# Linear attention and feed-forward on one core: w and u as single rows spread by PE, decay blocks by fp32 matmuls, a shared PSUM pool, unit loads one by one, weight slices gated one by one, dummy matmuls first

## The chip, the cores and the metric

The kernel runs on one core of a Trainium2 chip. The metric is the device time of one execution in microseconds (us), median of several runs. The engines are named as in the profile: PE (matmuls), PEld (weight loads of PE), DVE, ACT, POOL, SP; "SPq" and "POOLq" or a DMA_DIRECT2D row on POOL are the queues of an engine in the act of issuing a DMA.

## The reference

The reference is a linear-attention recurrence, followed by a feed-forward layer with a squared ReLU (cut to what matters):

```python
# r, k, v: (4, 8, 768, 48); w, u: (8, 48); w_in: (384, 2048); w_out: (2048, 384); all fp32
for t in range(S):
    cur = np.einsum('bhd,bhe->bhde', u[None] * kt, vt)
    y[:, :, t] = np.einsum('bhd,bhde->bhe', rt, state + cur)      # (r.(u*k)) v is the "diagonal" term
    state = w[None, :, :, None] * state + np.einsum('bhd,bhe->bhde', kt, vt)
...
h = np.maximum(x @ w_in, 0.0)          # x: y as 3072 tokens x 384
out = h * h @ w_out
```

## The kernel before

The sequence is cut into 24 units (6 chunks of 128 tokens, 4 batches). For a unit, r and k are scaled by decay tables (`Wt2`, `Wkhat`, from log w), transposed, and multiplied into a masked score block; PE forms Y and the state update; DVE adds the diagonal term `dv = v * sum(r*u*k)`. Two units make a group of 256 tokens for the feed-forward layer: eight hidden steps (L604, six matmuls each), and four output steps per unit (L638, four matmuls each). The eight weight slices (four of w_in, four of w_out) are cast to bf16 by DMAs that POOL issues.

The program does not fix the order of these steps by hand. It lists them as `Step`s with guessed durations, simulates the engines in `order_steps`, and emits the instructions in the order of the simulated starts. A buffer holds a pair of units:

```python
        else:                                   # a single unit's load
            x, i = item[0], int(item[1:])
            var = f"{x}P{i // 2}"
            def go(x=x, i=i, var=var):
                nc.sync.dma_start(out=ld[x][slot[var]][:, i % 2], in_=single[x][i % B, i // B])
            Ld[x, i] = st("ld" + item, "SP", 0.4, dma=1.04, prio=-150 + n, emit=go,
                          alloc=[(var, "ld" + x)] if i % 2 == 0 else [])
...
PLAN = dict(..., loads=['k0', 'r0', 'v0', 'ub', 'k1', 'r1', 'v1', 'wcol', 'kP1', 'rP1', 'vP1', 'kP2', ...],
            nprep=8, p1set=2, nT=8, nX=8, gates=[('v', 2), ('v', 2)], ...)
POOLS = dict(ldr=2, ldk=2, ldv=2, rk=6, P0=4, dv=3, vb=8, rkT=6, bank=3, bankH=3, bankO=2, ...)
```

Only units 0 and 1 are loaded singly here (`k0` ... `v1`); `kP1` is both units of pair 1 in one DMA. w comes as a broadcast to 128 partitions (`wb`, 192 KB), u likewise (`ub`), and once more as a column (`wcol`). `gates` says which load has to land before POOL issues weights: v of unit 2 for both halves.

## Time and profile before

| | before |
|---|---|
| timed median | 183.56 us (183.44 to 183.97) |
| profiled span | 180.6 us |
| PE busy | 160.6 us (89%) |
| first hidden-layer matmul | 27.48 us |
| first weight slice issued | 18.23 us |
| DMA packets under 512 B | 98,864 of 105,794 |

The page's second part, the span in 40 slices of 4.5 us, with the busy share of PE, the granted PE clock and the DMA engines in tenths:

```profile
PE   0344769899999999999999999999999999999991
PEclk9999999999999999999999999999999999999999
DMA  3999999999949649979799799897896255221102
```

PE is full from the eighth slice or so, and DMA from the second. The table of stretches (start and end in us, length, then busy us and instruction counts of PE, PEld, DVE, ACT, POOL, then clock, DMA share and GB/s) makes this exact:

```profile
0.00:27.40 27.40, 12.47 (x128) 8.62 (x129) 20.84 (x44) 10.89 (x18) 16.50 (x29) 1.00 0.99 182
27.40:38.30 10.90, 9.82 (x111) 7.95 (x109) 9.84 (x18) 10.14 (x19) 4.25 (x5) 1.00 1.26 187
38.30:177.10 138.80, 138.26 (x1357) 101.67 (x1356) 97.92 (x156) 95.98 (x179) 86.01 (x84) 1.00 0.74 153
```

From 38.3 us on, PE is idle for half a microsecond in all. What can be won is in the start. The timeline there (start us, us, engine, line, operation, tiles; in brackets the idle time before and what ended it):

```profile
17.66 0.63 POOL L364 COPY gate<-ldv 1x1 f32<-1x1 f32 x2
...
18.23 3.26 POOL L371 DMA_DIRECT2D W<-in_moe_w_in_dram  x4
...
23.21 0.61 PE L454 MATMUL bank<-rkT 48*128 48x128 bf16 x8 [1.10 <-ACT rkT L436]
...
27.48 1.83 PE L604 MATMUL bank<-xT,W 128*128 128x256 bf16 x12
...
29.25 0.40 PE L454 MATMUL bank<-rkT 48*128 48x128 bf16 x8
```

The gates open at 17.7 us, all eight weight slices are issued by 24.5, the first hidden step runs at 27.5. The two L454 lines are the same work, eight score matmuls, first at 0.61 us, six microseconds later at 0.40.

**PE time lost.** "Busy" hides slow and dummy matmuls, so I use a second measure below. Each kind of useful matmul gets the time by which it advances a busy PE, read from the timeline of this kernel late in the span: a hidden matmul 0.655/6 us, an output matmul 0.65/4, and the attention's small ones 0.03 to 0.057. Summed over the trace this is 152.5 us of work (151.6 in the changed kernel, which does two transposes fewer on PE). At a time t, "lost" is t minus the useful work begun by then. These are estimates from the trace, good to some tenths of a us. The kernel before has lost 16.7 us by 20 us, 23.4 by 45, and 24.4 at its end.

### The profile page before, as it was taken

To read this page: it belongs to the slowest core of one execution; us is meant where nothing else is said; L and a number is where in the kernel's file an instruction comes from. 1 tells how busy PE (TensorE), PEld (TensorE's weight loads), DVE (VectorE), ACT (ScalarE), POOL (GpSimd) and SP (SyncE) were. 2 spreads that over 40 slices of the span, in tenths; PEclk is the share of its full clock that TensorE was granted. 3 is DMA by queue.
4 is the path that set the end of the run, shared out by engine and by line. 5 is a ranking of instruction groups with operands and counts; after the bars stand their busy time and mean duration, and the time that the engine had idled before them with its cause. 6 is when DMAs were issued, how large, how long until landed. Compare 5 with 4: busy or idle time off the path is not lost.

```text
span 180.6 us, 4082 instructions
## 1 busy us (share of the span) xinstructions
PE 160.6 (89%) x1592; PEld 118.2 (65%) x1592; DVE 128.6 (71%) x216; ACT 117.5 (65%) x214; POOL 106.8 (59%) x116
## 2 busy tenths in 40 slices
PE   0344769899999999999999999999999999999991
PEld 0222557778766867758678677677686776777760
DVE  3399998997388838959979696778777889631310
ACT  2641528986793886827776758579298495496851
POOL 2346998024940999599879977986968980000000
PEclk9999999999999999999999999999999999999999
DMA  3999999999949649979799799897896255221102
GB/s 85 207 195 216 196 191 193 184 185 222 225 116 241 149 82 253 184 152 241 142 216 204 122 237 202 138 225 164 167 228 155 71 120 80 65 65 47 41 2 87
DMA packets 105794, 28.44 MB, mean 157 GB/s; under 512 B 98864, under 2 KB 105776, under 8 KB 105776
## 3 DMA queue, kind: packets, MB, share of 16 engines
q1 hardware_dynamic: 102064, 25.04, 68.1%
q0 software_dynamic: 3712, 3.15, 11.0%
q8 instruction: 12, 0.20, 0.5%
q14 instruction: 6, 0.05, 0.1%
HBM read 20.84 MB, written 4.72 MB: 142 GB/s over the span
## 4 chain that ended last, share of the span: by engine, by line
PE 79%; DVE 9%; DMA 4%; ACT 2%; SPq 2%; issue 1%; DVEq 0%
PE bank L638 34%; PE bank L604 32%; PE bank L454 4%; PE bank L483 3%; DMA ub<-in_u_dram 2%; DMA xT<-xs 2%; PE bank L478 2%; PE bank L429 2%; DVE rk L382 2%; SPq L351 2%; DVE xs L506 2%; DVE dv L411 2%; PE bank L495 2%; DVE Bm L467 1%; ACT rkT L436 1%
## 5 line engine op out<-in xcount | busy, mean ns | idle before, releaser
L618 ACT ACTIVATE hr<-bank 128x512 bf16<-128x512 f32 x96 | 55.9, 595 | 29.4 <-PE bank L604 27.6
L604 PE MATMUL bank<-xT,W 128*128 128x256 bf16 x576 | 73.8, 273 | 0.4 <-DVE hq L629 0.3
L638 PE MATMUL bank<-W,hq 128*128 128x384 bf16 x384 | 72.0, 326 | 0.0
L604 PEld LDWEIGHTS <-W 128*128 128x128 bf16 x576 | 55.0, 98 | 11.8 <-issue 0.9
L638 PEld LDWEIGHTS <-hq 128*128 128x128 bf16 x384 | 36.1, 98 | 19.3
L629 DVE TENSOR_TENSOR hq<-bank,hr 128x512 bf16<-128x512 f32 x48 | 32.6, 683 | 17.4 <-ACT hr L618 17.4
L467 DVE TENSOR_TENSOR Bm<-bank,maskJT 128x512 bf16<-128x512 f32 x48 | 31.1, 681 | 8.2 <-PE bank L454 8.1
L388 POOL TENSOR_TENSOR P<-ldr,ldk 128x384 f32<-128x384 f32 x24 | 28.2, 1177 | 9.9 <-DMA ldr<-in_r_dram 9.9
L528 POOL TENSOR_TENSOR S0W<-ts,WLm 128x384 bf16<-128x384 f32 x16 | 16.5, 1031 | 29.1 <-DVE ts L522 28.9
L626 ACT ACTIVATE hq<-hr 128x512 bf16<-128x512 bf16 x48 | 30.2, 630 | 1.1
L397 POOL TENSOR_TENSOR P<-P,ub 128x384 f32<-128x384 f32 x22 | 22.9, 1043 | 1.4
L411 DVE TENSOR_TENSOR dv<-ldv,du 128x384 f32<-128x384 f32 x24 | 21.2, 883 | 0.5
L506 DVE TENSOR_TENSOR xs<-bank,dv 128x384 bf16<-128x384 f32 x24 | 13.3, 555 | 11.1 <-PE bank L483 10.7
L651 ACT COPY os<-bank 128x384 f32<-128x384 f32 x24 | 11.4, 476 | 12.4 <-PE bank L638 12.1
L429 PE MATMUL bank<-identity,rk 128*128 128x128 bf16 x64 | 7.5, 273 | 10.5 <-DVE rk L382 10.2
L382 POOL TENSOR_TENSOR rk<-ldr,Wt 128x384 bf16<-128x384 f32 x16 | 16.6, 1040 | 0.1
L382 POOL TENSOR_TENSOR rk<-ldk,Wkhat 128x384 bf16<-128x384 f32 x16 | 16.0, 1002 | 0.0
L429 PEld LDWEIGHTS <-rk 128*128 128x128 bf16 x64 | 5.5, 120 | 12.4 <-DVE rk L382 11.5
L417 ACT CAST vb<-ldv 128x384 bf16<-128x384 f32 x24 | 11.6, 507 | 2.9 <-DMA ldv<-in_v_dram 2.9
L403 DVE TENSOR_REDUCE du<-P 128x8 f32<-128x384 f32 x24 | 13.0, 543 | 0.2 <-POOL P L397 0.2
L454 PE MATMUL bank<-rkT 48*128 48x128 bf16 x192 | 10.6, 233 | 2.5 <-ACT rkT L436 2.2
L483 PE MATMUL bank<-vb,Bm 128*128 128x48 bf16 x192 | 12.2, 189 | 0.4 <-DVE Bm L467 0.4
(40 smaller groups left out, 101.7 us busy)
## 6 DMA issues: line engine op xcount, KB each, us to landing
out_dram<-os SPq DMA_DIRECT2D x24, 192.0 KB, 2.6
ldk<-in_k_dram SPq DMA_DIRECT2D x11, 384.0 KB, 4.1
ldr<-in_r_dram SPq DMA_DIRECT2D x11, 384.0 KB, 5.0
ldv<-in_v_dram SPq DMA_DIRECT2D x11, 384.0 KB, 4.0
W<-in_moe_w_in_dram POOLq DMA_DIRECT2D x4, 384.0 KB, 8.9
W<-in_moe_w_out_dram POOLq DMA_DIRECT2D x4, 384.0 KB, 15.6
ldk<-in_k_dram SPq DMA_DIRECT2D x2, 192.0 KB, 4.2
ldr<-in_r_dram SPq DMA_DIRECT2D x2, 192.0 KB, 4.5
```

The costliest lines, as they stand in the source:

```text
L382: e.tensor_mul(rk[slot[f"rk{i}"]][:, j, :, 0:D], ld[x][slot[f"{x}P{i // 2}"]][:, i % 2], tab)
L388: nc.gpsimd.tensor_mul(P0b[slot[f"P0{i}"]], ld["r"][slot[f"rP{i // 2}"]][:, i % 2], ld["k"][slot[f"kP{i // 2}"]][:, i % 2])
L397: (nc.vector if eng == "DVE" else nc.gpsimd).tensor_mul(t, t, ub)
L411: nc.vector.tensor_mul(dvb[slot[f"dv{i}"]], ld["v"][slot[f"vP{i // 2}"]][:, i % 2], du_b)
L454: nc.tensor.matmul(heads(f"bA{i}{e}", "bank", 128)[:, hc, :], rkT[p0 : p0 + D, HP + hc, :], rkT[p0 : p0 + D, hc, :], start=True, stop=True ...
L467: nc.vector.tensor_mul(Bmb[slot[f"Bm{i}"]][:, e], heads(f"bA{i}{e}", "bank", 128), mask_b)
L483: nc.tensor.matmul(Y[:, hc, D * e : D * (e + 1)], Bm[:, e, hc, :], vb[:, 2 * hc + e, :], start=(c == 0), stop=True, skip_group_check=True,)
L604: nc.tensor.matmul(hp[:, fi, :], W1[s // 2][:, c, 128 * f : 128 * (f + 1)], xt[:, c, :], start=(c == 0), stop=(c == CCH - 1), skip_group_c ...
L618: nc.scalar.activation(hrb[slot[f"hr{g},{s}"]], hp, AF.Relu)
L626: nc.scalar.activation(hq, hr, AF.Square)
L629: nc.vector.tensor_mul(hq, hp, hr)
L638: nc.tensor.matmul(o, hqb[slot[f"hq{g},{f // 2}"]][:, f % 2, L * j : L * (j + 1)], W2[q][:, f % 4, :], start=(f == 0), stop=(f == FCH - 1) ...
```

## The change

The intent is to fill PE earlier: take the broadcasts off DMA, load the early units singly so that the weights may start sooner, let the weight slices come one by one, let PSUM banks go where they are needed, and run dummy matmuls while PE has nothing to do. Cut to its core (the rest of the long diff rewrites emit functions without changing what they emit):

```diff
-PLAN = dict(per=6.2, loads=['k0', 'r0', 'v0', 'ub', 'k1', 'r1', 'v1', 'wcol', 'kP1', 'rP1', 'vP1', 'kP2', ...
-   nprep=8, p1set=2, nT=8, nX=8, gates=[('v', 2), ('v', 2)], sq=(1, 3, 5, 7), ldlead=26, lead=-1, ...)
-POOLS = dict(ldr=2, ldk=2, ldv=2, rk=6, P0=4, dv=3, vb=8, rkT=6, bank=3, bankH=3, bankO=2, Bm=3, ...)
+PLAN = dict(per=6.2, loads=['k0', 'r0', 'v0', 'k1', 'r1', 'v1', 'k2', 'r2', 'v2', 'k3', 'r3', 'v3', 'k4', 'r4',
+   'v4', 'k5', 'r5', 'v5', 'kP3', ...], gates=[('v', 2), ('r', 3), ('r', 3), ('r', 3), ('r', 3), ('r', 3), ('v', 3),
+   ('v', 6)], sq0=(0, 2, 3, 5, 7), nprep=4, p0set=2, p1set=1, nT=6, nX=8, gsq=2, ldlead=14, lead=-2, ..., fill=24)
+POOLS = dict(ldr=2, ldk=2, ldv=2, ..., rk=4, P0=6, dv=3, vb=8, rkT=3, bank=6, Bm=4, bankH=4, bankO=4, ...)
...
+    nc.scalar.dma_start(out=rows[:, 0, :], in_=flat_row(w))       # one row of 1.5 KB each
+    nc.scalar.dma_start(out=rows[:, 1, :], in_=flat_row(u))
+    def spread(row, var):
+        nc.tensor.matmul(bank(var)[:, 0 : H * D], ones, rows[:, row, :], start=True, stop=True, ...)
+    def e_wlb():                                                  # decay blocks: 8 fp32 matmuls of 1x48
+        ...
...
# order_steps: any of the 8 banks for any use, within a limit for each use
+                if p.startswith("bank"):
+                    share[p] -= 1
+                    q = slots["banks"]
...
# still only the even unit of a pair asks for a buffer, but now for units 0 to 5
+            Ld[x, i] = st("ld" + item, "load", (x, i), "SP", 0.4, dma=0.85, prio=-150 + n,
+                          alloc=[(f"{x}P{i // 2}", "ld" + x)] if i % 2 == 0 else [])
...
# dummy matmuls where the simulation sees PE idle, up to 24 us
+            if s.start < min(opened, PLAN["fill"]):
+                cost = 0.45 if s.start < 5 else 0.24
+                for _ in range(int((s.start - before - 0.2) / cost)):
+                    nc.tensor.matmul(banks[7], warm[:, 0:128], warm, start=True, stop=True, ...)
```

## The prediction

> **What bounds the kernel now.** From 38.3 us on it is PE: in the stretch table PE is busy 138.3 of the 138.8 us from 38.3 to 177.1, and the chain of waits there is almost only PE (feed-forward lines L604 and L638, 66% of the span). Behind PE's end come a 0.48 us copy and the last store, to 180.6. So the span is PE's own work plus what PE loses before it is full. From the timeline one hidden step of six matmuls advances PE by 0.655 us and one output step of four by 0.65; 96 of each are 125 us, and the attention's matmuls bring it to about 152 us. PE ends at 177.1, so about 24.5 us are lost, nearly all before 27.5 us, when the first feed-forward matmul runs.
>
> That start is a DMA matter. From 5 to 45 us the 16 DMA engines are 101 to 128% busy at about 200 GB/s, and nearly all packets are under 512 bytes (98,864 of 105,794). One unit load of 192 KB takes about 1.1 us of them. The broadcast w and u are two such loads (landing 3.6 and 4.1 us after issue, u at 8.5). The weight slices are issued only from 18.2 us, after v of unit 2, which comes in a two-unit load; the first lands 6.7 us later, the last at about 42, one every 2.5 us.
>
> **What the change does.**
> 1. w and u as rows: two broadcasts and the 4-byte-packet column load leave DMA, about 2.5 us; k0, r0, v0 land some 1 us earlier. Against it stand two small fp32 matmuls of about 1 us each, one on the path to the decay tables: these come at best 0.5 us earlier (5.65 now).
> 2. Units 2 to 5 load singly, so v2 is the ninth load instead of part of the fourteenth: it should land near 12.5 us, not 17.6, and the first weight slice near 19 instead of 25. This is the main gain, about 6 us.
> 3. Each weight slice then feeds two groups (2.6 us of PE work per 2.5 us of DMA), with banks shared so that several accumulations can be open: PE should stay nearly full from about 20 us.
> 4. Dummy matmuls: a group of eight score matmuls takes 0.61 us at 23 us and 0.40 at 29, although the granted clock reads 1.00 throughout. The Trainium skill, "TensorE: Matmul & The Clock Gate" (Part 1), describes such a half-rate start, ended by sustained activity. That shortens early chain steps; perhaps 1 us.
> 5. Two transposes fewer on PE: 0.9 us. POOL takes over preparation of four units (2.04 us each, about 7 us net), DVE and ACT change by a few us; POOL was 59% busy, so this should hide.
>
> The tail stays at 3.5 us.
>
> **Sum.** First feed-forward matmul at 19 to 20 us, with 5 to 6 us of useful PE work before it: 14 us lost, plus 1.5 to 3 in the ramp. 151.6 + 16 + 3.5 is a span of 171.5; the timed median lies 3 us above the profiled span: 174 us.
>
> Predicted 174.0 us, range 169.5 to 179.0. Faster by over 2%: 0.91; same: 0.07; slower: 0.02.
>
> **What would show it.** First L604-type matmul near 20 us in the timeline; first weight slice issued near 13; PE slices full from the fifth or sixth on; eight-matmul groups at 0.4 us early; PE's last matmul near 168.
>
> **What would make it wrong.** Loads starve behind the weight slices, so that units 4 to 7 come late and PE has holes at 35 to 60 us; POOL, 5.3 us per unit against 6.2, becomes the pacemaker; or late weights (slice 7 waits for v6) hold the first outputs.

## The result

The changed kernel takes 195.84 us (median of 4, 194.42 to 196.75) against 183.74 us of the kernel before in the same rounds. The ratio is 1.065 (95% interval 1.059 to 1.072). Ratios in this document are the mean time of one kernel's fast runs over that of the other's of the same rounds, so not quite the ratio of the medians. The change made the kernel slower by 6.5%, where 5% faster was predicted.

The three rows of the page's second part, now of the changed kernel, each slice 4.9 us:

```profile
PE   7994000599999999999999999969999999999992
PEclk9999655579999999999999999999999999999999
DMA  6999999265624999979979599999799755210202
```

PE is idle from the fifth slice to the seventh, and the clock falls with it. Its stretch table:

```profile
0.00:15.00 15.00, 13.18 (x91) 6.42 (x93) 9.49 (x25) 7.85 (x14) 5.95 (x18) 1.00 0.96 181
15.00:35.00 20.00, 1.95 (x14) 0.63 (x13) 1.00 (x4) 1.42 (x3) 10.54 (x12) 0.64 1.14 180
35.00:45.00 10.00, 8.89 (x93) 6.75 (x94) 8.60 (x17) 4.77 (x9) 5.10 (x5) 0.70 0.40 79
```

Between 15 and 35 us PE, DVE and ACT do next to nothing for 20 us, while DMA is full. The start itself went as planned. These lines of the changed kernel's timeline answer to the ones shown of before (L518 is the gate, L522 the weights, L571 the scores, L647 the hidden layer):

```profile
10.88 0.40 PE L571 MATMUL bank<-rkT 48*128 48x128 bf16 x8
...
11.15 0.18 POOL L518 COPY gate<-ldv 1x1 f32<-1x1 f32 x1 [0.51 <-DMA ldv<-in_v_dram]
...
11.27 0.93 POOL L522 DMA_DIRECT2D W<-in_moe_w_in_dram  x1
...
40.47 1.05 PE L647 MATMUL bank<-xT,W 128*128 128x256 bf16 x6
```

v of unit 2 lands at 11.1 us instead of 17.6, the first weight slice leaves at 11.27 instead of 18.23, the scores run at the full rate from the first. And yet the first hidden matmul comes at 40.5 us. The wait list of PE (who waited for whom: us in total, times, longest) and DVE's timeline say where the chain broke:

```profile
PE bank L593 <- DVE Bm L581: 19.1, 2, 18.7
```

```profile
14.98 0.54 DVE L538 TENSOR_REDUCE du<-P 128x8 f32<-128x384 f32 x1
34.52 0.56 DVE L543 TENSOR_TENSOR dv<-ldv,du 128x384 f32<-128x384 f32 x1 [19.00 <-DMA ldv<-in_v_dram]
34.99 1.28 DVE L581 TENSOR_TENSOR Bm<-bank,maskJT 128x512 bf16<-128x512 f32 x2
```

PE waits for DVE's mask product, and DVE, on which nothing runs from 15.52 to 34.52 us, stands for 19.0 us before a `dv`. It is the second `dv` of the kernel, that of unit 1, and it waits for a load of v. But v of unit 1 had landed by 10.54 us, when ACT began to cast it. The load that it waits for is another, issued at 17.12 us; the chain of waits has it, and SP's timeline:

```profile
17.12 17.30 DMA ldv<-in_v_dram
...
34.52 0.56 DVE dv L543
```

```profile
17.12 8.31 SPq L510 DMA_DIRECT2D ldv<-in_v_dram  x2
```

**Which load is it?** The instruction lists of the two engines in the program as built (not a view of the trace), with the semaphores that each instruction waits for (the loads signal eight lanes in turn; DMAHW2 is the lane of the 17th load, and the load of v1, the 6th, has lane 7):

```
SP  17  DMACopy ldv_0<-in_v_dram 128x8x48 [waits DMAHW2, Activation]
SP  18  DMACopy ldv_0<-in_v_dram 128x8x48 [waits DMAHW3]
DVE 25  TensorReduce du_1<-P0_1
DVE 26  TensorTensor dv_1<-ldv_0,du_1 [waits DMAHW2, DVE]
```

In e1_fix below, the same DVE instruction reads `[waits DMAHW7, DVE]`. In the order that `order_steps` made, the steps come as `ldv5`, `dv1`, `ldv4`. Loads 17 and 18 are v of unit 5 and then of unit 4. Unit 4's load asks for a pair buffer, and with two buffers it has to wait until `dv1` gives one back. Unit 5's load asks for nothing, so the scheduler let it pass. Its buffer's number was filled in later, and it is the same buffer, `ldv_0`, second half: the half that still holds v of unit 1. So in program order the load of v5 stands *before* `dv1`, and the framework, which knows only program order, makes `dv1` wait for it. The wait is not needed for anything; worse, `dv1` then reads v of unit 5 where the reference wants v of unit 1: built again from its source, the program's load 17 fetches v from element 301,056 on (batch 1, tokens 128 to 255, which is unit 5) into the half at offset 384 of `ldv_0`, and `dv_1` reads that half. (The comparison accepted the result all the same. It only says accepted or not, so no run here measures the size of that error; that the wrong value is read follows from the built program, not from a result. Worked out with the reference on its own inputs, without the chip, that one wrong term changes the output by 1.5% in the norm of the whole and by 7.1% over unit 1's 128 tokens.) The wait makes it free of races.

**Why did that load take 17.5 us?** By then the weight slices were on the way. The DMA view of that stretch (17.2 to 34.4 us; packets, MB, share of 16 engines' time) in the changed kernel:

```profile
q0 software_dynamic: 2784, 2.36, 84.9%
q1 hardware_dynamic: 3828, 0.72, 31.4%
...
ldv<-in_v_dram SPq DMA_DIRECT2D x2, 192.0 KB, 17.5
```

The weights' queue q0 took most of the engines' time, and the loads in q1, the two of v and those issued just before them, got 0.72 MB through in 17 us, where they had moved 1.76 MB in the 8 us from 3 to 11 us. A single v load takes 3.5 us at the best, 17.5 us here. The Trainium skill ("Trainium Kernel Development and Optimization", Key Constraints) says that DMAs of all issuing engines share the same 16 DMA engines, and "DMA: Bandwidth & Descriptors" (Queues, rings and completion order) that each of them takes turns between its queues packet by packet. The trace fits: the packet counts are of one order (2,784 to 3,828), the bytes are 3.3 to 1 in favour of the queue with the larger packets.

The clock is a smaller part: PE was busy for 3.89 of the 5 us from 35 to 40 us, so half the clock cost some 2 us there (an estimate). The Trainium skill, "TensorE: Matmul & The Clock Gate" (Part 1), says that an idle window puts PE's clock back to half. The trace agrees: the granted clock is 0.50 from 25 to 40 us, and the score group at 39.92 us takes 0.61 us again.

### The profile page after: what moved, and what is told of

The parts are those of the page before. It is cut to its first block, busy times and chain, and to the rows that moved or that the text cites. A ratio compares the mean times of both kernels' runs of the same rounds, so it can differ in the third digit from the quotient of the medians.

```text
span 194.3 us, 4172 instructions
## 1 busy us (share of the span) xinstructions
PE 167.0 (86%) x1621; PEld 119.3 (61%) x1623; DVE 118.6 (61%) x206; ACT 119.4 (61%) x216; POOL 112.1 (58%) x123
## 4 chain that ended last, share of the span: by engine, by line
PE 64%; DMA 15%; POOL 7%; DVE 3%; SPq 2%; issue 1%; ACT 0%; DVEq 0%; POOLq 0%
PE bank L647 27%; PE bank L669 26%; DMA ldv<-in_v_dram 9%; DMA rkT<-rk 6%; PE bank L571 3%; POOL rk L528 3%; PE bank L593 2%; POOL P L531 2%; PE bank L589 2%; POOL S0W L623 2%; SPq L510 1%; POOL P L535 1%; PE bank L602 1%; PE bank L555 1%; PE bank L698 1%; DVE xs L610 1%
## 5 line engine op out<-in xcount | busy, mean ns | idle before, releaser
L647 PE MATMUL bank<-xT,W 128*128 128x256 bf16 x576 | 75.3, 273 | 0.0
L669 PE MATMUL bank<-W,hq 128*128 128x384 bf16 x384 | 73.8, 326 | 0.0
L647 PEld LDWEIGHTS <-W 128*128 128x128 bf16 x576 | 54.9, 98 | 12.5 <-issue 0.2
L669 PEld LDWEIGHTS <-hq 128*128 128x128 bf16 x384 | 35.9, 98 | 18.0
L664 DVE TENSOR_TENSOR hq<-bank,hr 128x512 bf16<-128x512 f32 x46 | 31.4, 686 | 21.6 <-ACT hr L657 21.3
L581 DVE TENSOR_TENSOR Bm<-bank,maskJT 128x512 bf16<-128x512 f32 x48 | 31.2, 686 | 17.4 <-PE bank L571 15.4
L662 ACT ACTIVATE hq<-hr 128x512 bf16<-128x512 bf16 x50 | 31.6, 632 | 1.2
L543 DVE TENSOR_TENSOR dv<-ldv,du 128x384 f32<-128x384 f32 x24 | 18.6, 774 | 19.6 <-DMA ldv<-in_v_dram 19.0
L535 POOL TENSOR_TENSOR P<-P,ub 128x384 f32<-128x384 f32 x23 | 23.4, 1016 | 9.1 <-DVE P L531 7.5
L528 POOL TENSOR_TENSOR rk<-ldk,Wkhat 128x384 bf16<-128x384 f32 x20 | 20.2, 1011 | 14.3 <-PE bank L602 14.3
L531 POOL TENSOR_TENSOR P<-ldr,ldk 128x384 f32<-128x384 f32 x22 | 23.6, 1072 | 0.0
L593 PEld LDWEIGHTS <-Bm 128*128 128x128 bf16 x192 | 9.8, 97 | 20.5 <-DVE Bm L581 19.7
L558 ACT COPY rkT<-bank 128x1024 bf16<-128x1024 bf16 x6 | 6.1, 1010 | 26.5 <-PE bank L555 26.5
L528 POOL TENSOR_TENSOR rk<-ldr,Wt 128x384 bf16<-128x384 f32 x20 | 21.6, 1080 | 0.0
L571 PE MATMUL bank<-rkT 48*128 48x128 bf16 x192 | 9.7, 222 | 2.8 <-DMA rkT<-rk 2.5
```

The costliest lines, as they stand in the source:

```text
L528: engine(e).tensor_mul(rk[slot[f"rk{i}"]][:, j, :, 0:D], unit(x, i), tab)
L531: engine(e).tensor_mul(P0b[slot[f"P0{i}"]], unit("r", i), unit("k", i))
L535: engine(e).tensor_mul(t, t, ub)
L543: nc.vector.tensor_mul(dvb[slot[f"dv{i}"]], unit("v", i), du_b)
L581: nc.vector.tensor_mul(Bmb[slot[f"Bm{i}"]][:, e], heads(f"bA{i}{e}", 128), mask_b)
L593: nc.tensor.matmul(Y[:, hc, D * e : D * (e + 1)], Bm[:, e, hc, :], vb[:, 2 * hc + e, :], start=(c == 0), stop=True, skip_group_check=True,)
```

## The experiments

Eleven runs of nine kernels were made, in three calls (e1 to e4; e5, e6, e8 and e9; e7, e10 and e11). The chips differed, and with them the kernel before: its medians were 184.69, 183.18 and 183.44 us. So kernels are compared by their ratio to the kernel before. The third call had no run of e1_fix, and e1_fix itself moved by 0.8% from the first call to the second; smaller differences between calls say nothing. All were accepted as correct. The lost PE time, as defined above, of each profiled run, and the ratio with its 95% interval (e2_nodummy is left out, as its times are unclear):

| kernel | by 20 us | by 30 us | by 45 us | at the end | median us | ratio to before |
|---|---|---|---|---|---|---|
| before | 16.7 | 21.7 | 23.4 | 24.4 | 183.74 | 1 |
| changed kernel | 16.8 | 26.8 | 35.9 | 38.7 | 195.84 | 1.065 (1.059 to 1.072) |
| e1_fix | 15.7 | 17.4 | 17.7 | 21.4 | 178.94 | 0.970 (0.962 to 0.978) |
| e4_late_weights | 16.8 | 22.2 | 22.3 | 28.9 | 185.77 | 1.008 (0.997 to 1.018) |
| e3_gates_v2 | 14.8 | 16.7 | 25.0 | 29.2 | 185.90 | 1.005 (0.995 to 1.016) |
| e8_fix_again (= e1_fix) | 15.7 | 16.9 | 17.8 | 19.4 | 176.23 | 0.962 (0.959 to 0.966) |
| e5_bufs | 15.7 | 16.4 | 17.7 | 18.6 | 176.20 | 0.963 (0.958 to 0.968) |
| e6_broadcast | 16.1 | 18.0 | 19.9 | 21.5 | 178.63 | 0.975 (0.972 to 0.978) |
| e9_nodummy_again | 14.7 | 16.7 | 18.0 | 22.0 | 178.56 | 0.972 (0.968 to 0.976) |
| e7_pairs | 15.0 | 18.7 | 19.0 | 21.5 | 178.95 | 0.976 (0.973 to 0.980) |
| e10_ldv3 | 15.7 | 17.6 | 17.7 | 23.7 | 180.29 | 0.983 (0.977 to 0.988) |
| e11_banks | 16.1 | 18.6 | 20.1 | 24.1 | 181.46 | 0.990 (0.985 to 0.996) |

### e1_fix: a pair's second load waits until the pair has its buffer

Two theories stood against each other. A: the load of v5 in the wrong place makes `dv1` wait. B: the early weights starve the loads of units 4 and 5 whatever the order, and mending the order only moves the hole.

```diff
-    def __init__(s, name, kind, ..., shared=False):
+    def __init__(s, name, kind, ..., shared=False, need=None):
+        s.need = need
...
+                if s.need and s.need not in where:      # in order_steps: buffer not given out yet
+                    fits = False
...
                           alloc=[(f"{x}P{i // 2}", "ld" + x)] if i % 2 == 0 else [],
+                          need=f"{x}P{i // 2}" if i % 2 else None)
```

The edit moves little else: of the 906 steps in the order that `order_steps` makes, the first 169 differ from the changed kernel's only in the places of `ldv4` and `ldv5`.

> The changed kernel with one rule more for its scheduler: the second unit of a pair buffer may be loaded only once the pair's buffer has been given out, so the load of v for unit 5 comes after that of unit 4, hence after unit 1's dv product has read the old v. Theory A (false order): in the changed kernel v5 was put in program order ahead of dv1 into the half buffer that dv1 reads, so dv1 waited 19.0 us for a load that lay behind the weights (and used the wrong v). Then here dv1 waits under 1 us, PE has no hole over 3 us between 15 and 35 us, the first hidden-layer matmul comes at 19 to 22 us (40.5 in the changed kernel), the time is 172 to 178 us, and the error against the reference falls. Theory B (plain starvation: early weights keep the loads of units 4 and 5 away, whatever the order): v4 and v5 still land only near 34 us, the hole only moves to about 22 to 35 us, and the time stays above 184 us.

Measured: 178.94 us (four runs, one of them slow), ratio 0.970 (0.962 to 0.978), clearly faster than both kernels. Where the changed kernel stood for 19 us, DVE in e1_fix goes on:

```profile
15.19 0.54 DVE L542 TENSOR_REDUCE du<-P 128x8 f32<-128x384 f32 x1
15.76 0.56 DVE L547 TENSOR_TENSOR dv<-ldv,du 128x384 f32<-128x384 f32 x1
```

SP's issue of the same two loads, and the first hidden matmul, in e1_fix's timeline:

```profile
18.49 8.22 SPq L514 DMA_DIRECT2D ldv<-in_v_dram  x2
...
21.01 0.81 PE L651 MATMUL bank<-xT,W 128*128 128x256 bf16 x6
```

The stretch of 15 to 35 us in e1_fix's stretch table:

```profile
15.00:35.00 20.00, 18.45 (x191) 12.69 (x191) 17.30 (x29) 14.40 (x25) 15.46 (x17) 1.00 1.24 197
```

Theory A holds. The hidden layer starts at 21.0 us instead of 40.5. And B's premise is true but harmless: the two v loads are as late as ever. They are issued from 18.49 us on, and the chain of waits of e1_fix has 17.06 us for the landing of the first, till 35.55:

```profile
18.49 17.06 DMA ldv<-in_v_dram
```

But in the right order only units 4 and 5 need them, and PE is full with groups 0 and 1 until then: from 15 to 35 us PE is busy for 18.45 us (dummies included) and has lost only 2 us more by 45 us than at 20. The time missed the expected 172 to 178 us by 1 us. Whether the error fell could not be seen, as the comparison gives no size.

### e4_late_weights: the wrong order kept, the weights after v5

If the length of the stall is the landing time of v5, the stall must shrink when nothing stands in that load's way.

```diff
-gates=[('v', 2), ('r', 3), ('r', 3), ('r', 3), ('r', 3), ('r', 3), ('v', 3), ('v', 6)]   # changed kernel, no new rule
+gates=[('v', 5)]*8
```

> The changed kernel with its wrong order kept (v5 ahead of dv1), but all weight slices released only when v5 has landed. Theory A says the length of the stall is the landing time of v5: not behind weights it lands near 18 us, so dv1's wait shrinks from 19.0 us to 2 to 5 us, the first hidden-layer matmul comes near 27 us and the time is 179 to 186 us, though the result stays as wrong as the changed kernel's. If the stall had another cause than that load, it stays near 19 us.

Measured (2 runs): 185.77 us, ratio 1.008. DVE's timeline in e4_late_weights:

```profile
14.36 0.54 DVE L538 TENSOR_REDUCE du<-P 128x8 f32<-128x384 f32 x1
19.30 0.56 DVE L543 TENSOR_TENSOR dv<-ldv,du 128x384 f32<-128x384 f32 x1 [4.39 <-DMA ldv<-in_v_dram]
```

The same wrong wait is there, at 4.4 us instead of 19.0, and the first hidden matmul comes at 27.65 us as expected. (The weights leave 8 us later here, at 19.37 us, which also holds up the hidden layer; so it is the wait of `dv1`, and not the time, that this run tests.) So the loss is a product of two things: the false order says *that* `dv1` waits for v5, and the weights on the same DMA engines say *how long*.

### e10_ldv3: the changed kernel with a third v buffer

The same theory, tested by a change of one number and without the new rule: with a third pair buffer the load of v4 never waits, so v5 has nothing to overtake and no half in use to write into.

```diff
-POOLS = dict(ldr=2, ldk=2, ldv=2, ...)
+POOLS = dict(ldr=2, ldk=2, ldv=3, ...)
```

> The changed kernel as it came, without the new rule, but with three pair buffers for v instead of two: one number. v4 and v5 then go into a third buffer, so no load can get ahead of a reader of its half. Theory A (false order into a shared half buffer): dv1 no longer waits for v5, no PE hole over 3 us between 15 and 35 us, ratio to the kernel before 0.955 to 0.985, as with e1_fix. If the stall had come from something else in the order of the changed kernel, it stays, and the ratio stays near 1.06.

Measured: 180.29 us, ratio 0.983, in the range. In e10_ldv3's timeline the second `dv` follows its `du` at once:

```profile
15.81 0.54 DVE L538 TENSOR_REDUCE du<-P 128x8 f32<-128x384 f32 x1
16.38 0.83 DVE L543 TENSOR_TENSOR dv<-ldv,du 128x384 f32<-128x384 f32 x1
```

The first hidden matmul comes at 21.34 us. By 45 us it has lost 17.7 us of PE, as e1_fix has. That it ends slower (0.983 against 0.962 to 0.970) comes later: in the profiled run PE stands idle for 3.0 us up to 64.1 us before a score group whose transposes come by DMA. The extra early v loads change the order of SP's queue; I did not pursue this.

### e3_gates_v2: all weights at once

With the order mended, is it worth anything to hold the slices back one by one?

```diff
-gates=[('v', 2), ('r', 3), ('r', 3), ('r', 3), ('r', 3), ('r', 3), ('v', 3), ('v', 6)]
+gates=[('v', 2)]*8
```

> e1_fix with all eight weight slices released by v of unit 2, as the kernel before released its own (there v2 landed later). If holding slices back one by one is worth something, the loads of units 3 to 7 land later here, and it is 1 to 4 us slower than e1_fix. If only the early release counts, within 1 us of it.

Measured: 185.90 us, ratio 1.005, in the same call as e1_fix's 0.970: 3.5% or 6.4 us of 184.69, more than either answer expected. Two stretches of e3_gates_v2, and then the largest entry of PE's wait list:

```profile
30.00:35.00 5.00, 1.95 (x16) 1.13 (x14) 1.68 (x3) 2.09 (x4) 1.00 (x1) 1.00 1.27 186
35.00:40.00 5.00, 2.72 (x12) 1.55 (x13) 0.71 (x2) 1.94 (x3) 2.94 (x3) 0.58 1.09 212
```

```profile
PE bank L559 <- POOL rk L532: 6.2, 3, 4.9
```

Here theory B's hole is real. Released together the weights hold back k and r of units 4 and 5 (POOL's scaling waits 4.3 us for a load of r in the timeline), and PE, which has nothing left of groups 0 and 1, loses 8 us between 30 and 45 us. In e1_fix POOL waits 2.9 us for the same load, r of unit 5, and goes on at 30.49 instead of 36.23 us; its PE loses 0.3 us from 30 to 45 us.

### e2_nodummy and e9_nodummy_again: without dummy matmuls

```diff
-fill=24
+fill=0
```

> e1_fix without the dummy matmuls, all else in the same order. If the dummies shorten the start, eight-matmul score groups before 20 us take 0.61 us instead of 0.40 and the time is 0.5 to 2 us above e1_fix. If they are neutral (PE waits for others anyway), within 0.5 us of it. If they delay real work, below e1_fix.

> e2_nodummy again beside its partner. Its trace (though of a slow run) had lost 14.6 us of PE by 20 us against 15.7 with dummies, and 17.1 against 17.0 by 25 us: the dummies take PE from real work about as much as the full clock gives back. So within 1 us of e8_fix_again. If the dummies are worth their place, 1 to 2 us above it.

The first try is inconclusive: two of its four runs were in the slow state, the other two took 178.22 and 180.34 us, and the verdict is unclear (0.972, interval 0.960 to 0.984). The second (six runs, one slow) gave 0.972 (0.968 to 0.976) against 0.962 (0.959 to 0.966) of its partner. So leaving the dummies out costs 1.0%, 1.8 us, and the last expectation was missed. That the dummies give the full rate is plain in the traces: without them the score groups before 20 us take 0.61 us each, with them 0.40, and the 128-column transposes start 107 ns apart until 16.6 us, where with dummies (e8_fix_again) they start some 56 ns apart from 9.1 us on. My reason for expecting less than 1 us still holds where it was made: without dummies the kernel has lost 14.7 us by 20 us against 15.7 with them (they stand in the way of real work), and by 45 us the two are equal within 0.3 us. In the profiled runs the difference arises after 45 us, in DMA holes that differ from run to run, and the profiled run without dummies was a slow one. What links dummies before 24 us with holes after 45 us I can't say; that stays open.

### e6_broadcast: w and u as broadcasts again

```diff
     def e_wrow():
-        pass                                      # the row came by ACT's queue
+        nc.sync.dma_start(out=wb..., in_=flat_rows(w))
     def e_urow():
+        nc.sync.dma_start(out=ub..., in_=flat_rows(u))
     def e_wbb(): / e_ubb(): / e_ub():
-        spread(0, "bw") / spread(1, "bu") / nc.scalar.copy(ub..., bank("bu")...)
+        pass
...                                               # e_logw reads wb; the rows' two DMAs go
```

> e1_fix with w and u loaded as before, as two 192 KB broadcasts ahead of the units, and PE not spreading them. By the trace of the kernel before, such a load holds DMA for about 1 us: v2 lands about 2 us later, the first weight slice too, and the time is 1 to 3 us above e1_fix. If the rows are worth nothing (the loads wait on other things), within 0.5 us.

> e1_fix again, as the partner of the other runs of this call: 178 to 180 us in its fast runs, 0.97 of the kernel before.

Measured: 0.975 against 0.962, 1.3% or 2.3 us. The lost time by 45 us is 2.1 us more, and v of unit 2 opens its gate at 13.13 us instead of 11.20. The rows do what they were meant to do. The partner, e8_fix_again, is e1_fix at 176.23 us, below its expected 178 to 180; that its ratio moved from 0.970 to 0.962 between two chips shows how far ratios can be trusted.

### e5_bufs: the old number of transpose buffers

```diff
-rk=4, rkT=3
+rk=6, rkT=6
```

> e1_fix with the old numbers of transpose buffers: rk 6 instead of 4, rkT 6 instead of 3. In e1_fix PE still loses 3.7 us after 40 us (1.0 in the kernel before), in holes whose releaser is a DMA: a transpose or a weight slice. If the transposes come late because the change left them fewer buffers, the holes at 95 to 100 and 130 to 137 us (2.9 us together) mostly go and it is 1.5 to 3 us faster than e1_fix. If they come late because DMA is full or because the preparation on POOL is late, the holes stay and it is within 1 us of e1_fix.

Measured: 0.963 against 0.962 of e8_fix_again. No gain from the buffers: they are not what costs the time of the later holes. The holes themselves move and change size between runs of one kernel (after 45 us e1_fix lost 3.7 us in one profiled run, 1.6 in another), and what ends them is mostly a DMA transpose.

### e7_pairs and e11_banks: single loads and shared banks

```diff
-'k2', 'r2', 'v2', 'k3', 'r3', 'v3', 'k4', 'r4', 'v4', 'k5', 'r5', 'v5', 'kP3'     # e7_pairs
+'kP1', 'rP1', 'vP1', 'kP2', 'rP2', 'vP2', 'kP3'
```

> e1_fix with units 2 to 5 loaded in pairs of 384 KB, as the kernel before did, gates and all else by the same rules. The prediction credited the single loads with most of the gain (v2 ninth in the queue instead of within the twelfth). If so, the first hidden-layer matmul moves from 21 to 23.5 to 25 us and the time is 2 to 4 us above e1_fix. If the broadcasts' removal and the gates carried it, within 1 us.

Measured: 0.976, so 0.6 to 1.4% slower than the two runs of e1_fix. They were run at other times. The intervals of this run and of the first e1_fix overlap, so a cost of the pairs is not shown; it is 1.4% at most by these means. The mechanism expected is refuted: v of unit 2 does open its gate later, at 14.23 us instead of e1_fix's 11.51, but r of unit 3 opens its gate earlier (12.40 instead of 13.87), and the first hidden matmul comes at 19.7 us, earlier than e1_fix's 21.0. What PE loses, it loses later: 1.8 us before weight slices at 24.5 and 26.9 us, and 1.7 us up to 30.4 us before a transpose whose scaling on POOL is late.

```diff
-bank=6, bankH=4, bankO=4                                                          # e11_banks
+bank=3, bankH=3, bankO=2
```

> e1_fix with the kernel before's limits on PSUM banks (3 for attention, 3 for hidden, 2 for output, adding up to 8, so nothing is shared any more) in place of 6, 4 and 4 out of a common 8. If the shared pool lets PE go on during the ramp while weight slices arrive one by one, PE has lost 2 to 4 us more by 45 us and the time is 2 to 4 us above e1_fix; if it is worth nothing, within 1 us.

Measured: 0.990, 2.0 to 2.8% slower than e1_fix; by 45 us PE has lost 20.1 us against 17.7. The shared pool is worth 3.7 to 5.1 us (of 183.44) here, the largest part but the gates and at the upper end of the expected 2 to 4 us or above it. This edit, like those of the loads and gates, also changes the order that `order_steps` makes, so each is worth what it is worth *in that order*.

## Why the prediction was wrong

**The step that failed** is number 3, "PE should stay nearly full from about 20 us", because number 2 took the single loads as a mere gain of landing time. In the changed kernel PE was busy for 1.95 of the 20 us from 15 to 35 us, and the first hidden matmul came at 40.5 us instead of 19 to 20. I read the list of loads and the buffer counts, but not the rule by which the second unit of a pair takes its buffer. With units 4 and 5 loaded singly and only two pair buffers, the rule let the load of v5 be emitted ahead of the last reader of that half. Shown: the 19.00 us wait of `dv1` on a load of v (changed kernel), its fall to 4.4 us when that load is fast (e4_late_weights), and its absence when the order is mended by a rule (e1_fix) or by a third buffer (e10_ldv3). Read from the built program and not shown by a result: that `dv1` also reads the wrong v.

The prediction's own list of dangers came near and missed: it named loads starved behind the weight slices, with holes at 35 to 60 us for want of units 4 to 7. The starving was real (17.5 us for a 192 KB load), but harmless by itself in e1_fix; it became 19 us only through unit 1, which did not need the load at all.

Point by point, for the rest:

- *What bounds the kernel* was right in the main. PE's own work, 151.6 us, and the time lost by 45 us make most of the span in all these kernels; another 0.9 to 6.6 us are lost after 45 us.
- *Rows instead of broadcasts*: right. The first decay table is ready at 5.11 us (4.50 + 0.61) instead of 5.65, and the rows are worth 2.3 us (e6_broadcast), predicted about 2.5 us of DMA.
- *v2 near 12.5 us, first slice out near 13*: 11.1 and 11.27 us, right and even better. "This is the main gain, about 6 us" was not: pairs cost 0.6 to 1.4%, which is not clear of the noise (e7_pairs). The gates (6.4 us, e3_gates_v2) and the banks (some 4 us, e11_banks), which the prediction put into one sentence, carry more. Such parts don't add up: the five sum to 15 to 18 us, and the whole mended change wins 5.5 to 7.
- *Dummies, perhaps 1 us*: 1.8 us measured, and the early groups did run at 0.40 us; but in the profiled runs nothing is left of it by 45 us, so that the early chain doesn't explain the gain: the size is near the forecast by luck, and by which way it pays is open.
- *POOL hides its extra work*: mostly right, POOL is busy 58% of the changed kernel's span, though it makes up 7% of its chain of waits, where the kernel before had none of it worth a line.
- *The sum*: "14 us lost, plus 1.5 to 3 in the ramp" was 15.5 to 17 us for a kernel without the false order. In e1_fix it is 17.7 by 45 us, and another 1.6 to 3.7 us in DMA holes that I had put at zero. Hence 176 to 179 us where 174 was predicted: the mended kernel lies in the upper part of the range, and the kernel as it was given 17 us above its end.

The best kernel is e1_fix, the change with the rule added: 3.0 to 3.8% faster than before, and 16.9 us below the median of the change as it came (178.94 against 195.84 us).

## What to carry to other kernels

When instructions are emitted in an order that a program computes, every step that writes into a shared buffer must ask for it; one that doesn't can be placed ahead of the last reader, and the framework will faithfully wait for the wrong data, free of races and, here, within tolerance. In a trace, look at an engine's longest wait and ask whether the instruction needs what it waits for: a `dv` of unit 1 that waits for a load issued after unit 1's v had landed is a false dependency, whatever bandwidth it seems to lack. And move bulk transfers earlier only with an eye on who shares the DMA engines: 192 KB took 3.5 us at the best among the other loads and 17.5 us beside the weights.

## What the Trainium skill lacked or had wrong

- "DMA: Bandwidth & Descriptors" (Queues, rings and completion order) gives the taking of turns packet by packet but no figure for what it means when one queue has small packets. Here: 2.36 MB for the weights' queue and 0.72 MB for the loads' in 17.2 us, and a 192 KB load stretched from 3.5 to 17.5 us.
- "TensorE: Matmul & The Clock Gate" (Part 1) describes the half-rate start rightly (in the kernel before, 128-column transposes start 107 ns apart until 26.6 us and 56 ns apart from 30.9 us on; eight score matmuls take 0.61 us and then 0.40), and warns that the records of the clock can't be fully trusted. What is missing is how this looks: in the kernel before, the granted clock reads 1.00 through the whole slow start, and only after a long idle stretch (changed kernel, 25 to 40 us) does it show 0.50.
- The same page's table of advice has PE kept busy for some 4 us to get the full clock; it does not say that dummies stand in line with real work. Here PE had done 1.0 us less useful work at 20 us with them than without (15.7 against 14.7 us lost); by 45 us the two were equal within 0.3 us.
- No page warns of a wait that is correct by program order and wrong by intent; it cost 19.0 us here.
